# First two groups of chunks: fp32 operands, unscaled K, and products with T and A on 32x32 tiles

## The chip, the cores and the metric

The kernel runs on one core of a Trainium2 chip. The metric is device time in microseconds (us), smaller is better; the median of several runs counts. The engines are PE (TensorE: matmuls and weight loads), DVE (VectorE), ACT (ScalarE), POOL (GpSimd) and SP, which here only issues DMA transfers. "us" of an engine are its busy time in a profiled execution.

## The reference

A delta-rule attention over 4 batches x 8 heads, 768 tokens, 48 dimensions per head, followed by a gated feed-forward network on its output:

```python
k_n = k / (np.linalg.norm(k, axis=-1, keepdims=True) + 1e-06)
state = np.zeros((B, H, D, D))
for t in range(S):
    y[:, :, t] = q[:, :, t] @ state                    # per head
    v_old = state^T k_n[:, :, t]
    state = state + beta_t * outer(k_t, v_t - v_old)
x = y as [B*S, H*D] = [3072, 384]
out = ((x @ w_a) * (x @ w_b)) @ w_out                  # w_a, w_b: 384 x 1536, w_out: 1536 x 384
```

All inputs and outputs are fp32. Only the recurrence over t is sequential; the network works on each token alone.

## The kernel before, in words

**Chunks and groups.** The 768 tokens are cut into 24 chunks of 32 tokens, and the chunks into 6 groups of 4. The 32 pairs of batch and head are worked on at once: 4 blocks of 32 partitions times 8 column blocks q. Within a chunk the recurrence is replaced by products: with A the strictly lower triangle of Q K^T, and T the inverse of a unit triangular matrix made from K K^T times the strengths beta, a chunk takes the old state S, forms `ks` = K S, then vt = V - ks, then u = T vt, then `yp` = Q S + A u, and adds K^T u to the state in PSUM (`S_ps`). So each chunk waits for the state of the chunk before.

**Three stages per group.** `prep(g)` computes the squares and norms of K and Q, loads K and Q with tokens along the columns (`kqt` into `raw`), multiplies K there by the reciprocal of its norm (`rbk` or its slice `rb`, spread over the partitions: in group 0 by a matmul, in the others through a small array `rk` in DRAM), lays K and Q out in block-diagonal tiles `kqbd`, and makes the products K K^T and K Q^T (in the trace `raw,kqbd` for fp32, `kqc,kqbd` for fp16). `solve(g)` inverts the triangular matrices with 31 short VectorE steps (group 0: 15 steps on two halves at once, then small matmuls `b,ta`, `b,mk` and `wr,b`). `steps(g)` walks through the chunks: `shl` is the copied state, `khl` K with tokens along the partitions, `uhl` u, `t` vt, `y` the output of the chunk. The matmul with T is `t,tabd` (fp32) or `fhl,tabd` (fp16), the one with A is `uhl,tabd`. `tabd` is a block-diagonal 128x128 copy of the 32x32 matrices, made from the tile `ta` by copies on ScalarE and VectorE, whose split the table `COPY` holds ('AVAV': one letter per piece). Those of `kqbd` come likewise.

**Precision.** In general every attention operand is split into two fp16 halves, high and low, and a product is a sum of three fp16 products (`parts(g)`). Groups with `WIDE[g]` = 1, before this change group 0 alone, use fp32 operands and one product instead; a tile in fp32 takes the room of its two fp16 halves (`half`, `ta32`, `tas32`). The low half of a tile is made by one VectorE instruction, or, where `VIA_PE` names it by letter, by a matmul with a negative identity `neg` (in the trace `raw,mk` and `kqc,neg`, `t,mk` and `khl,neg`) whose result ScalarE copies. `LO_W` does the same for the three column thirds of the weights ('P': matmuls `wsl,zi` and `wsl,neg`; 'V': VectorE).

**The feed-forward stage.** `weights(p)` decodes a third of the weights and splits it into high and low fp16 halves (`wsl`, `wos`). Two chunks together make one piece of x (256 tokens, `x`), and `moe(s, ths)` runs per block of 128 hidden columns 18 matmuls 128x256 (`x,wsl`), ACT and DVE instructions that make the gate `g` and its halves `ghl`, and 6 matmuls 128x384 (`wos,ghl`). The latter come `LAG` blocks later. There are 144 such blocks.

**What sets the order.** No engine's order stands in the source. `Plan` records every operation, prices each (`price`), links them by what they read and write, and places them by list scheduling with priorities (`URGENCY` by stage) under several settings, of which it issues the one that it reckons shortest. Every instruction is issued at one line, and so has L476 in the trace. Each engine, and SP's queue of transfers, runs its instructions in that fixed order; an instruction that waits holds up those behind it. The pool of 6 PSUM banks and the rings of tiles (`raw`, `t`, `b`, `tabd`) are shared among the stages.

## Time and profile before

| | |
|---|---|
| median of 3 runs | 673.44 us (672.57 to 675.61) |
| profiled execution: device time, span | 675.9 us, 674.1 us |
| PE, DVE, ACT, POOL busy | 621.5, 545.0, 400.2, 11.5 us |
| first product of the first solve on PE | at 58.85 us |
| first MoE matmul on PE | at 107.95 us |
| first MoE matmul with x of the second group | at 215.52 us |

Times are of one profiled execution, in us from the start of its span. A row of groups reads: line, engine, operation, output <- inputs, shapes, count, then busy time in us and the mean of one in ns, then the idle time just before and what released it. A row of the timeline reads: start, length, engine, operation, count, idle before it. An fp32 matmul leaves two matmul records or one, by its form, so counts of records are not counts of calls. `PEclk` is the granted clock of PE as a share of full speed, in tenths in the slices of the page.

### The profile page before, as it was taken

The numbers are of one execution on the slowest core, as the hardware profiler recorded it, in microseconds if no ns is written. First come the engines' busy times: TensorE is split into PE (matmuls) and PEld (weight loads), VectorE is DVE, ScalarE is ACT, GpSimd is POOL, SyncE is SP. The second block draws the span as 40 slices with busy tenths as digits, with TensorE's granted clock in tenths as the row PEclk, the third lists the DMA queues.
The fourth block names the chain that finished last, engine by engine and source line by source line (L and its number), as shares of the span: only waits on it lengthen the run. The fifth ranks groups of instructions, "written<-read, shape, count | busy, mean of one in ns | idle before, by whom it ended". The sixth has DMA issues, their size and how long they took to land.

```text
span 674.1 us, 24273 instructions
## 1 busy us (share of the span) xinstructions
PE 621.5 (92%) x10578; PEld 495.0 (73%) x10578; DVE 545.0 (81%) x1532; ACT 400.2 (59%) x968; POOL 11.5 (2%) x15
## 2 busy tenths in 40 slices
PE   0748989999989999999999999999999999999997
PEld 0524878787777888777777778888777878887885
DVE  5999669899998799989999798899897898644232
ACT  9679548975387565477733876525657235553332
POOL 0000011100000000000000000000000000000000
PEclk9967659999999999989999999999999999999999
DMA  8997635512231432202420023001222000000000
GB/s 313 342 328 220 197 119 176 157 52 71 64 97 47 141 95 76 59 26 78 135 63 25 3 83 104 26 1 44 83 65 63 13 13 27 26 26 1 13 13 23
DMA packets 30243, 59.10 MB, mean 88 GB/s; under 512 B 3386, under 2 KB 21050, under 8 KB 30138
## 3 DMA queue, kind: packets, MB, share of 16 engines
q1 hardware_dynamic: 30138, 57.57, 27.2%
q8 instruction: 82, 1.34, 0.9%
q14 instruction: 23, 0.19, 0.1%
HBM read 52.75 MB, written 4.80 MB: 85 GB/s over the span
## 4 chain that ended last, share of the span: by engine, by line
PE 49%; DVE 32%; ACT 10%; DMA 6%; issue 2%; DVEq 0%; ACTq 0%; SPq 0%
PE bank L476 47%; DVE b L476 6%; DVE tmp L476 4%; DMA raw<-in_kqt 3%; DVE g L476 3%; DVE ghl L476 2%; DVE wsl L476 2%; DVE kqc L476 2%; ACT kqbd L476 2%; ACT tabd L476 2%; PE S_ps L476 2%; DVE t L476 2%; DVE wos L476 1%; DVE shl L476 1%; ACT t L476 1%
## 5 line engine op out<-in xcount | busy, mean ns | idle before, releaser
L476 PE MATMUL bank<-x,wsl 128*128 128x256 f16 x2592 | 309.8, 273 | 1.0 <-DVE x L476 0.8
L476 PEld LDWEIGHTS <-wsl 128*128 128x128 f16 (+1 forms) x2676 | 255.5, 98 | 61.1 <-DVE wsl L476 16.6
L476 PE MATMUL bank<-wos,ghl 128*128 128x384 f16 x864 | 165.3, 327 | 1.4 <-issue 1.2
L476 PEld LDWEIGHTS <-ghl 128*128 128x128 f16 x864 | 81.5, 98 | 41.3 <-issue 0.8
L476 ACT CAST ghl<-g 128x256 f16<-128x256 f32 x144 | 58.4, 405 | 83.5 <-DVE g L476 82.5
L476 ACT ACTIVATE a<-bank,rsc 128x256 f32<-128x256 f32 x120 | 56.8, 473 | 76.9 <-PE bank L476 76.3
L476 DVE TENSOR_TENSOR g<-bank,a 128x256 f32<-128x256 f32 x144 | 60.4, 420 | 47.3 <-ACT a L476 46.9
L476 DVE TENSOR_TENSOR ghl<-g,ghl 128x256 f16<-128x256 f32 x144 | 60.4, 419 | 17.6 <-ACT ghl L476 17.1
L476 PEld LDWEIGHTS <-kqbd 112*64 112x64 f16 x2880 | 51.6, 114 | 15.7 <-issue 13.4
L476 DVE TENSOR_TENSOR b<-b,tmp 128x31 f32<-128x31 f32 (+20 forms) x170 | 56.3, 331 | 2.1
L476 DVE TENSOR_TENSOR tmp<-b 128x31 f32<-128x31 f32 (+20 forms) x170 | 56.1, 330 | 2.1
L476 PE MATMUL bank<-shl,kqbd 112*64 112x48 f16 (+1 forms) x2112 | 46.6, 195 | 2.1 <-DVE shl L476 1.7
L476 ACT ACTIVATE t<-bank 128x96 f32<-128x96 f32 x96 | 22.6, 249 | 22.6 <-PE bank L476 22.1
L476 PEld LDWEIGHTS <-tabd 128*128 128x128 f16 x960 | 28.6, 96 | 7.9 <-issue 4.4
L476 DVE COPY tabd<-ta 32x1024 f16<-32x1024 f16 (+1 forms) x64 | 26.8, 419 | 5.9 <-ACT ta L476 3.0
L476 ACT COPY tabd<-ta 32x1024 f16<-32x1024 f16 (+1 forms) x32 | 29.7, 930 | 0.4
L476 ACT ACTIVATE t<-bank,y 128x96 f32<-128x96 f32 x96 | 25.6, 343 | 7.1 <-DVE y L476 7.0
L476 PE MATMUL bank<-uhl,tabd 128*128 128x48 f16 (+1 forms) x544 | 27.1, 203 | 2.4 <-issue 1.9
L476 ACT ACTIVATE ld<-ld 128x1536 f32<-128x1536 f32 x15 | 22.3, 1488 | 9.2 <-DMA ld<-in_vn 5.1
L476 PE MATMUL S_ps<-uhl,khl 32*48 32x48 f16 (+1 forms) x2080 | 23.6, 191 | 2.1 <-issue 1.9
L476 DVE COPY kqbd<-kqc 48x2048 f16<-48x2048 f16 x32 | 21.9, 684 | 1.8 <-PE bank L476 1.5
L476 PE MATMUL bank<-wsl 128*128 128x128 bf16 (+1 forms) x84 | 8.2, 236 | 15.9 <-DVE wsl L476 15.9
(154 smaller groups left out, 789.4 us busy)
## 6 DMA issues: line engine op xcount, KB each, us to landing
raw<-in_kqt SPq DMA_DIRECT2D x21, 448.0 KB, 3.7
rbk<-rk SPq DMA_DIRECT2D x40, 128.0 KB, 3.1
t<-in_kn SPq DMA_DIRECT2D x24, 192.0 KB, 2.7
stage<-in_wo SPq DMA_DIRECT2D x6, 768.0 KB, 5.8
out<-wsl SPq DMA_DIRECT2D x24, 192.0 KB, 1.9
ld<-in_kn SPq DMA_DIRECT2D x5, 768.0 KB, 7.8
ld<-in_qtok SPq DMA_DIRECT2D x5, 768.0 KB, 5.5
ld<-in_vn SPq DMA_DIRECT2D x5, 768.0 KB, 6.2
```

The source lines that it names most:

```text
L476: fn(*(self.place(a, lease) for a in args), **{k: self.place(a, lease) for k, a in kw.items()})
```

## The change

- The second group joins the first in `WIDE`: fp32 operands, one product in place of three.
- In both, T and A are multiplied as 32x32 tiles straight from the tile `ta` (`TILED_T`, in `ta_of`), so that no block-diagonal copies `tabd` are made for them.
- K stays unscaled there. The squares of the reciprocal norms go into the strengths (`bs`), and v is multiplied by the factors `r` (`vt`) with `ks` added afterwards; the product with the broadcast reciprocals goes, and with it the detour over DRAM of group 1 and the matmul of group 0. `k32` is loaded straight into `khl`. The inverse gets a factor of 2^18 that keeps its range.
- `VIA_PE` is empty, and `LO_W` is 'VVV': all low halves come from VectorE.
- `LAG` is 3 in place of 2. `COPY` is set anew for K of group 0, T of groups 1 and 4. Priorities of `prep0` and `steps1` rise.
- In the planner, the prices of fp32 matmuls change, and the transfers with a rank (`first_of`) go first on SP's queue, in the order of their ranks, with all the others behind.

```diff
@@ -30,30 +30,34 @@
-COPY = {'k': ['AA', 'AA', 'VV', 'VV', 'VV', 'VV'], 'ta': ['AVAV', 'AVAV', 'AVAV', 'AVAV', 'VVVV', 'VVVV']}
+COPY = {'k': ['VV', 'AA', 'VV', 'VV', 'VV', 'VV'], 'ta': ['AVAV', 'AVVV', 'AVAV', 'AVAV', 'AVAV', 'VVVV']}
 TILED_K = [0, 0, 0, 0, 0, 0]
-TILED_T = [0, 0, 0, 0, 0, 0]
-VIA_PE = ['aknu', 'kn', '', '', '', '']
+TILED_T = [1, 1, 0, 0, 0, 0]
+VIA_PE = ['', '', '', '', '', '']
...
-WIDE = [1, 0, 0, 0, 0, 0]
+WIDE = [1, 1, 0, 0, 0, 0]
+TILED_G = [0, 0, 0, 0, 0, 0]
 WD = 512
-LO_W = 'PVV'
-LAG = 2
+LO_W = 'VVV'
+LAG = 3
 LEAD = 4
-URGENCY = {'w0': 100, 'w0b': 800, 'w1': 300, 'w2': 300, 'prep0': 1000, 'solve0': 400, 'steps0': 300, 'prep1': 600, 'solve1': 200, 'steps1': 100, 'prep': 200, 'solve': 600, 'steps': 500, 'moe': 800, 'moe_pe': 300}
+URGENCY = {'w0': 100, 'w0b': 800, 'w1': 300, 'w2': 300, 'prep0': 1100, 'solve0': 400, 'steps0': 300, 'prep1': 600, 'solve1': 200, 'steps1': 200, 'prep': 200, 'solve': 600, 'steps': 500, 'moe': 800, 'moe_pe': 300}
 class Op:
-    __slots__ = ("eng", "calls", "dur", "move", "rd", "wr", "deps", "pri", "at", "end", "tag", "stream", "banks", "cold", "use", "many")
+    __slots__ = ("eng", "calls", "dur", "move", "rd", "wr", "deps", "pri", "at", "end", "tag", "stream", "banks", "cold", "use", "many", "rank")
...
         self.cold, self.use, self.many = 0.0, 0.0, 0
+        self.rank = None
         self.rd, self.wr, self.deps, self.tag, self.banks = {}, {}, set(), "", set()
@@ -74,6 +78,11 @@
         self.behind = set()
+        self.rank = None
+    def first_of(self, rank):
+        self.rank = rank
@@ -169,11 +178,13 @@
                 if ins[0].dtype == F32:
-                    return n if k <= 32 else 1.3 * n
+                    return 28.0 if k <= 48 else 66.0
                 return 10.0 if k <= 32 else 19.0
...
                 return 34.0 + n / 2.4
-            return (max(n, 60) / 2.4 + 2.3) * (4 if ins[0].dtype == F32 else 1)
+            if ins[0].dtype == F32:
+                return (max(n, 134) / 2.4 + 2.3) * 4
+            return max(n, 60) / 2.4 + 2.3
         if eng == "ACT":
...
@@ -414,7 +428,8 @@
             for k, late in nxt[i]:
-                ready[k] = max(ready[k], end + late)
+                ready[k] = max(ready[k], stop[i] if late is None else end + late)
                 left[k] -= 1
@@ -449,6 +464,14 @@
                 self.pred[i].append((j, late))
+        front = sorted((i for i, o in enumerate(ops) if o.rank is not None), key=lambda i: ops[i].rank)
+        for i, k in zip(front, front[1:]):
+            self.succ[i].append((k, None))
+            self.pred[k].append((i, None))
+        for k, o in enumerate(ops):
+            if o.eng == "SP" and o.rank is None:
+                self.succ[front[-1]].append((k, None))
+                self.pred[k].append((front[-1], None))
         best = None
...
@@ -806,6 +827,8 @@
     def ta_of(g, c, rows, which, l, q):
+        if WIDE[g] and TILED_T[g]:
+            return tas32(c, which)[rows, q]
         if WIDE[g]:
@@ -835,10 +858,13 @@
         if g == 0:
+            plan.first_of(1)
             SP.dma_start(kn0, kn[0:4].rearrange("c p d -> p c d"))
...
             V.tensor_reduce(ss, kn0.rearrange("p c (q e) -> p (c q) e", e=D), AX.X, ALU.add)
+            plan.first_of(0)
             load_raw(0, raw0)
+            plan.first_of(2)
             SP.dma_start(raws[0:KR], kqt[1:4].rearrange("c d x -> d c x"))
@@ -857,14 +883,14 @@
         rT = rTt
-        V.transpose(rT, r)
-        if g == 0:
-            for t, e in zip(ar.tiles, (rch[:, 0:4], rch[:, 4:8])):
-                A.copy(t.rearrange("p (k d) -> p k d", d=64), e.unsqueeze(2).broadcast_to([P, 4, 64]))
-            V.tensor_mul(
-                rbk0, rT.unsqueeze(1).broadcast_to([P, 16, 32]), rpi.unsqueeze(2).broadcast_to([P, 16, 32])
-            )
+        if WIDE[g]:
+            bs = bsm[:, g * 32 : g * 32 + 32]
+            V.tensor_mul(r, r, r)
+            V.tensor_mul(bs, bs, r)
+            V.transpose(bun[:, g * 32 : g * 32 + 32], bs)
         else:
+            V.transpose(rT, r)
             rk = scr.tile([2, 32, 2, 32], F32, name=f"rk{g}")
@@ -892,6 +918,9 @@
         V.tensor_scalar_mul(sc[:, 0:1], sc[:, 5:6], -256.0)
+        if WIDE[g]:
+            V.tensor_scalar_mul(r, s1, sc[:, 0:1])
         if g:
@@ -909,26 +938,16 @@
                 load_raw(c, rw)
+            if not WIDE[g]:
                 src = rk[:, ci * 8 : ci * 8 + 8].rearrange("h u r t -> h (u r t)")
...
                     )
-            else:
-                rb = abr()
-                T.matmul(
-                    rb,
-                    ar.tiles[ci // 2][:, ci % 2 * P : ci % 2 * P + P],
-                    rbk0.rearrange("p a t -> p (a t)"),
-                    start=True,
-                    stop=True,
-                )
-                rb = rb.rearrange("p (a t) -> p a t", t=32)
             bd = kqbd[c % 4]
             if WIDE[g]:
-                V.tensor_mul(rw[0:KR, 0], rw[0:KR, 0], rb[0:KR])
                 b32 = kq32(c)
-                for k in range(2 if c else 1):
+                for k in range(2) if c else [0] * (not TILED_G[g]):
                     for h2 in range(2):
...
@@ -988,7 +1008,9 @@
         (G if g else V).memset(X, 0.0)
-        V.tensor_copy(X.rearrange("p t s -> p (t s)")[:, 0 : 33 * 31 + 1 : 33], bun[:, g * 32 : g * 32 + 32])
+        V.tensor_scalar_mul(
+            X.rearrange("p t s -> p (t s)")[:, 0 : 33 * 31 + 1 : 33], bun[:, g * 32 : g * 32 + 32], 2.0**18 if WIDE[g] else 1.0
+        )
         size = 16 if HALVES[g] else 32
@@ -1064,16 +1086,13 @@
             bd, ta, tab = kqbd[c % 4], tas[c], tabd[c % 2]
-            kn32 = s15()
             khl = khr()
-            k32 = half(khl) if WIDE[g] else kn32
-            SP.dma_start(kn32, kn[c])
-            V.tensor_mul(
-                k32.rearrange("p (q e) -> p q e", e=D),
-                kn32.rearrange("p (q e) -> p q e", e=D),
-                r[:, ci * 8 : ci * 8 + 8].unsqueeze(2).broadcast_to([P, 8, D]),
-            )
+            k32 = kn32 = half(khl) if WIDE[g] else s15()
+            SP.dma_start(k32, kn[c])
+            rb = r[:, ci * 8 : ci * 8 + 8].unsqueeze(2).broadcast_to([P, 8, D])
+            by_heads = lambda t: t.rearrange("p (q e) -> p q e", e=D)
             if not WIDE[g]:
+                V.tensor_mul(by_heads(kn32), by_heads(kn32), rb)
                 k2 = khl.rearrange("p l q e -> p l (q e)")
@@ -1096,9 +1115,11 @@
             f32 = vt
-            if first:
+            if WIDE[g]:
+                V.tensor_mul(by_heads(vt), by_heads(v0), rb)
+            elif first:
                 A.activation(vt, v0, AF.Copy, scale=sc[:, 5:6])
-            else:
+            if not first:
                 if ci == 0:
@@ -1119,7 +1140,10 @@
                         )
-                V.scalar_tensor_tensor(vt, v0, sc[:, 0:1], ks[:, 0:384], op0=ALU.mult, op1=ALU.add)
+                if WIDE[g]:
+                    V.tensor_add(vt, vt, ks[:, 0:384])
+                else:
+                    V.scalar_tensor_tensor(vt, v0, sc[:, 0:1], ks[:, 0:384], op0=ALU.mult, op1=ALU.add)
             fhl = None if WIDE[g] else fhr()
@@ -1144,7 +1168,7 @@
             if WIDE[g]:
-                A.activation(u32, up[:, 0:384], AF.Copy, scale=2.0**-10 if first else -(2.0**-18))
+                A.activation(u32, up[:, 0:384], AF.Copy, scale=-(2.0**-18))
             else:
...
```

SP's queue, first rows, before:

```order
L476 DMA wsl<-in_kn 128x4x384
L476 DMA b_70<-in_wa 128x1024
L476 DMA stage<-in_wa 128x2x1024
L476 DMA ld_75<-in_kn 128x4x384
L476 DMA b_70<-in_wb 128x2x1024
L476 DMA mk<-in_masks 128x444
L476 DMA raw_110<-in_kqt 112x1024
L476 DMA wsl<-in_kqt 112x3x1024
```

and after (`kqt` are K and Q, `kn` K with tokens along partitions, `wa` and `wb` weights):

```order
L499 DMA raw_111<-in_kqt 112x1024
L499 DMA wsl<-in_kn 128x4x384
L499 DMA wsl<-in_kqt 112x3x1024
L499 DMA b_70<-in_wa 128x1024
L499 DMA stage<-in_wa 128x2x1024
L499 DMA b_70<-in_wb 128x2x1024
L499 DMA t_0_71<-in_beta 128x192
L499 DMA acc<-in_vn 128x4x384
L499 DMA mk<-in_masks 128x420
```

K and Q of the first four chunks have moved from behind the weights to the front, and the masks behind them.

PE, in the steps of the first group's early chunks, before (`bank_...` are the PSUM banks; the shapes are those of the outputs):

```order
L476 MATMUL bank_66<-b_70,ta_82 32x16 x32
L476 MATMUL bank_67<-b_70,mk 128x256
L476 MATMUL bank_65<-raw_110,mk 112x512
L476 MATMUL bank_64<-t_3_74,tabd_107 128x48 x8
L476 MATMUL bank_67<-wr_144,b_70 16x16 x32
L476 MATMUL bank_68<-uhl_151,tabd_107 128x48 x8
L476 MATMUL S_ps<-uhl_151,khl_145 48x48 x32
L476 LDWEIGHTS neg_117
L476 MATMUL bank_65<-kqc_80,neg_117 112x512
```

and after:

```order
L499 MATMUL S_ps<-uhl_152,khl_146 48x48 x32
L499 MATMUL bank_66<-b_70,ta_83 32x16 x32
L499 MATMUL bank_64<-shl_148,kqbd_105 64x48 x16
L499 MATMUL bank_68<-b_70,mk 128x256
L499 MATMUL bank_67<-uhl_152,ta_81 32x48 x32
L499 MATMUL bank_65<-t_1_72,ta_82 32x48 x32
L499 MATMUL bank_66<-b_70,ta_84 32x16 x32
L499 LDWEIGHTS mk
L499 MATMUL bank_67<-y_0_123,mk 128x4
```

The 8 products with `tabd`, each over the whole array, have become 32 products of 32x32 tiles with `ta`; the products `raw,mk` and `kqc,neg`, which made low halves for the second group, are no longer there.

More of the change, by code (lines that the diff above doesn't have):

```diff
@@ L215, in add @@
         if eng == "SP":
+            op.rank, self.rank = self.rank, None
             op.dur = 430.0
@@ L232, in add @@
                 else:
-                    op.cold += max(outs[0].shape[-1] if len(outs[0].shape) == 2 else 64, 48) / 1.2 * (4 if ins[0].dtype == F32 else 1)
+                    wide = ins[0].dtype == F32
+                    n = outs[0].shape[-1] if len(outs[0].shape) == 2 else 64
+                    op.cold += max(n, 131 if wide else 48) / 1.2 * (4 if wide else 1)
         for regs, aps in ((op.wr, outs), (op.rd, ins)):
@@ L526, in tile_kernel @@
     one = lambda name, shape, dt=F32: cst.tile(shape, dt, name=name)
-    mk = cst.tile([P, 60 + 3 * P], F32, name="mk")
+    mk = cst.tile([P, 36 + 3 * P], F32, name="mk")
     SP.dma_start(mk, masks)
@@ L532, in tile_kernel @@
     ones = mk[:, 32 : 32 + P]
-    rpi, rch = mk[:, 32 + 2 * P : 48 + 2 * P], mk[:, 48 + 2 * P : 56 + 2 * P]
-    same = mk.bitcast(BF16)[:, 2 * (56 + 2 * P) + 1 : 2 * (56 + 3 * P) : 2]
-    rown = mk[:, 56 + 3 * P : 60 + 3 * P]
+    same = mk.bitcast(BF16)[:, 2 * (32 + 2 * P) + 1 : 2 * (32 + 3 * P) : 2]
+    rown = mk[:, 32 + 3 * P : 36 + 3 * P]
     wsl = cst.tile([P, 19, 512], F32, name="wsl")
@@ L756, in heads, with pairs @@
                     yield q, i, l, rr, h4, slice(q * D, q * D + D)
-    def pairs(g):
+    def pairs(g, tiled=None):
         for q in range(8):
@@ L764, in pairs @@
                     cols = slice(q * D, q * D + D)
-                    if TILED_K[g]:
+                    if TILED_K[g] if tiled is None else tiled:
                         for h2 in range(2):
@@ L954, in prep @@
             with plan.group():
-                for q, i, l, rr, pr, rows, to, _ in pairs(g):
+                for q, i, l, rr, pr, rows, to, _ in pairs(g, TILED_G[g] if WIDE[g] else None):
+                    a = q * 2 + pr
                     T.matmul(
                         ga[to, q, :],
-                        kq_of(g, c, rows, l, q * 2 + pr, 0),
-                        rw[0:KR, :, q * 2 + pr] if WIDE[g] else kqc[rows, rr, q * 2 + pr],
+                        rw[rows, 0, a] if TILED_G[g] and WIDE[g] else kq_of(g, c, rows, l, a, 0),
+                        rw[rows, :, a] if WIDE[g] else kqc[rows, rr, a],
                         start=(i == 0),
@@ L1223, in steps @@
             if WIDE[g] and not WIDE[g + 1]:
-                G.memset(half(bd).rearrange("p (x n) -> p x n", n=64)[:, :, 16:48], 0.0)
-                if ci >= len(chs) - 2:
+                if c or not TILED_G[g]:
+                    G.memset(half(bd).rearrange("p (x n) -> p x n", n=64)[:, :, 16:48], 0.0)
+                if ci >= len(chs) - 2 and not TILED_T[g]:
                     G.memset(half(tab).rearrange("p (x n) -> p x n", n=128)[:, :, 16:112], 0.0)
@@ L1410, in _layout @@
                 perm[j * 128 + hp * 32 + e] = ((cc // D) * 4 + hp) * D + cc % D
-    masks = np.zeros((P, 60 + 3 * P), np.float32)
+    masks = np.zeros((P, 36 + 3 * P), np.float32)
     masks[:, 0:32] = np.tile(np.triu(np.ones((32, 32), np.float32), 1), (4, 1))
@@ L1415, in _layout @@
     masks[:, 32 + P : 32 + 2 * P] = np.eye(P, dtype=np.float32)
+    masks[:, 32 + 2 * P : 32 + 3 * P] = np.tile(np.eye(32, dtype=np.float32), (4, 4))
     row = np.arange(P)
-    masks[row, 32 + 2 * P + row % 8 * 2 + row // 64] = 1.0
-    masks[row, 48 + 2 * P + row // 8 % 4 * 2 + row // 32 % 2] = 1.0
-    masks[:, 56 + 2 * P : 56 + 3 * P] = np.tile(np.eye(32, dtype=np.float32), (4, 4))
-    masks[row, 56 + 3 * P + row // 32] = 1.0
+    masks[row, 32 + 3 * P + row // 32] = 1.0
     return {
```

## The prediction

> **What bounds the kernel now.** I read the page first: busy time, the slices, the granted clock.
>
> ```profile
> span 674.1 us, 24273 instructions
> PE 621.5 (92%) x10578; PEld 495.0 (73%) x10578; DVE 545.0 (81%) x1532; ACT 400.2 (59%) x968; POOL 11.5 (2%) x15
> PE   0748989999989999999999999999999999999997
> PEclk9967659999999999989999999999999999999999
> ```
>
> PE is busy in 621.5 of 674.1 us and idle mostly at the start; its clock is low in the third to sixth slice. Next the busy time by stage. The boundaries are the first product of the first solve (58.8), the first MoE matmul (107.9) and the first matmul of the second group's MoE (215.4).
>
> ```profile
> 0.00:20.00 20.00, 3.06 (x17) 1.96 (x18) 11.73 (x25) 18.91 (x33) 0.20 (x4) 1.00 0.91 309
> 20.00:57.00 37.00, 25.03 (x207) 13.85 (x206) 35.34 (x110) 26.82 (x39) 0.95 (x1) 0.82 0.98 328
> 58.80:107.90 49.10, 45.18 (x977) 38.41 (x977) 34.52 (x100) 30.94 (x70) 1.90 (x2) 0.63 0.53 164
> 107.90:215.40 107.50, 103.09 (x1627) 82.21 (x1626) 101.32 (x308) 76.80 (x175) 5.62 (x5) 1.00 0.30 92
> 215.40:674.10 458.70, 444.31 (x7764) 358.49 (x7758) 360.25 (x989) 244.88 (x651) 2.85 (x3) 0.99 0.16 49
> 187.00:215.00 28.00, 24.60 (x695) 18.96 (x695) 23.89 (x64) 23.34 (x58) 0.95 (x1) 1.00 0.26 76
> 140.00:187.00 47.00, 46.59 (x386) 37.12 (x384) 47.00 (x150) 24.87 (x54) 0.00 (x0) 1.00 0.16 49
> 300.00:320.00 20.00, 19.18 (x599) 15.50 (x597) 18.62 (x49) 15.33 (x46) 0.00 (x0) 1.00 0.25 74
> ```
>
> The columns are window, length, busy time (and records) of PE, weight loads, DVE, ACT, POOL, then granted clock, DMA share, GB/s. There are four regimes. Before 58.8 VectorE and the DMA are full (35.34 of 37 us, DMA share 0.98) and PE waits for the first solve. From 58.8 to 107.9 PE is busy for 45.18 of 49.10 us at a granted clock of 0.63, with small products. From there PE is at 96 to 97%; but from 140 to 187, while the second solve runs, VectorE has 47.00 of 47.00 us, so both bind. So the end is the start of the solve's products, plus the stretch ahead of the MoE, plus PE's work after it. The change touches all three.
>
> The profiled execution took 675.9 us with a span of 674.1, so 1.8 lie around it; the runs' median is 673.44, 2.5 below that execution. I sum against the span and set the result against the median.
>
> **Term 1, up to 58.8.**
>
> ```profile
> 6.84 0.43 DVE L476 TENSOR_SCALAR wsl<-b 128x512 int32<-128x512 int32 x1 [5.13 <-DMA b<-in_wa]
> 54.35 1.24 DVE L476 STREAM_TRANSPOSE b<-b 128x1024 f32<-128x1024 f32 x1
> 58.34 0.58 PE L476 MATMUL bank<-wsl,neg 128*128 128x512 f16 x1 [0.88 <-ACT wsl L476]
> 58.85 1.05 PE L476 MATMUL bank<-b,ta 32*32 32x16 f32 x64
> L476 DVE TENSOR_TENSOR wsl<-wsl,bank 112x512 f32<-112x512 f32 x3 | 2.0, 653 | 0.0
> raw<-in_kqt SPq DMA_DIRECT2D x21, 448.0 KB, 3.7
> wsl<-in_kqt SPq DMA_DIRECT2D x1, 1344.0 KB
> ```
>
> K and Q of the first four chunks (448 + 1344 = 1,792 KB) now go ahead of w_a. At 309 GB/s that delays w_a by 5.8 us, so its first decode starts near 12.6. VectorE, which is full here, loses the multiplications of K (three at 0.65, a fourth like them, the broadcast product: 3.3 us) and gains eight copies of K from ScalarE, 5.2 us at the same 0.65: +1.9. The solve's last transposition ends at 55.6 now, and PE's first product of it starts only at 58.85, behind `wsl,neg`, which waits for ScalarE. That product of the weights goes, so up to 3.2 us of lateness costs nothing here; 5.8 + 1.9 that isn't made good would cost 4.5. K is loaded before the weights and the first solve needs no K that is scaled, which can only bring it forward. Bounds -3 and +6; I take +1.
>
> **Term 2, 58.8 to 107.9.** The groups of this window, and single rows of the timeline:
>
> ```profile
> L476 PE MATMUL bank<-t,tabd 128*128 128x48 f32 x48 | 9.1, 366 | 0.0
> L476 PE MATMUL bank<-uhl,tabd 128*128 128x48 f32 x32 | 7.3, 415 | 0.0
> L476 PE MATMUL bank<-raw,mk 112*112 112x512 f32 x4 | 3.9, 1085 | 0.0
> L476 PE MATMUL bank<-wsl,neg 128*128 128x512 f16 x3 | 1.8, 606 | 0.9 <-ACT wsl L476 0.9
> L476 PE MATMUL bank<-kqc,neg 112*112 112x512 f16 x2 | 1.3, 654 | 0.0
> L476 PE MATMUL bank<-kqc,kqbd 112*64 112x64 f16 x96 | 2.4, 219 | 0.0
> 24.26 1.15 PE L476 MATMUL bank<-raw,kqbd 112*64 112x64 f32 x32
> 74.69 1.53 PE L476 MATMUL S_ps<-uhl,khl 32*48 32x48 f32 x64
> 112.99 0.93 PE L476 MATMUL S_ps<-uhl,khl 32*48 32x48 f32 x64
> 86.39 0.43 PE L476 MATMUL bank<-wr,b 32*16 32x16 f32 x30 [3.26 <-issue]
> 107.95 2.13 PE L476 MATMUL bank<-x,wsl 128*128 128x256 f16 x18
> ```
>
> The six groups all leave or change form: 9.1 + 7.3 + 3.9 + 1.8 + 1.3 + 2.4 = 25.8 us. In come the products with T and A on 32x32 tiles. Their nearest row is the state's product, also 32 fp32 tiles of 48 columns: 1.53 us for 64 records at the low clock, 0.93 at the full one. Three T and two A products (48 and 32 records of 16) thus become 5 x 1.53 = 7.7. Two products of K with K and Q, fp32 instead of three fp16 products, come at 1.15 each, 2.3. PE's work is then 45.2 - 25.8 + 10.0 = 29.4 us: 49.1 - 29.4 = 19.7 less if PE never waits for its instructions.
>
> But the records grow: 185 leave, 5 x 64 + 2 x 32 = 384 come, so some 1,180 matmuls, and as many weight loads: 2,350 records in place of 1,954. The densest sustained stretch of the trace is 300 to 320, 599 + 597 records in 20 us, 16.7 ns each. At that rate 2,350 take 39 us. The trace also shows PE idle for 3.26 us with the releaser "issue" in the middle of the densest run of small tiles. So the stretch lies between 29 (work) and 49 us (nothing gained); I take 39, **-10**.
>
> The Trainium skill's page "Runtime: NRT & Kernel Launch", section "Instruction fetch mechanics", says that the sequencer fetches blocks of 256 instructions ahead of itself and that this is mostly hidden; by that rule the stretch would be PE's own work, -20. The stall of 3.26 us speaks against the rule here, which is why it is a rival below.
>
> The cover of small products here is nothing: no MoE matmul can run before 107.95, so each us of waiting is one of the span.
>
> **Term 3, 107.9 to 215.4.**
>
> ```profile
> L476 PE MATMUL bank<-uhl,tabd 128*128 128x48 f32 x32 | 4.0, 277 | 0.0
> L476 PE MATMUL bank<-t,tabd 128*128 128x48 f32 x18 | 2.4, 277 | 0.0
> L476 PE MATMUL bank<-t,mk 128*128 128x384 f32 x8 | 3.3, 499 | 0.3 <-DVE g L476 0.3
> L476 PE MATMUL bank<-khl,neg 128*128 128x384 f16 x4 | 1.3, 334 | 0.0
> L476 PE MATMUL bank<-raw,mk 112*112 112x512 f32 x2 | 1.0, 593 | 0.0
> L476 PE MATMUL bank<-shl,kqbd 112*64 112x48 f16 x240 | 4.7, 190 | 0.0
> L476 PE MATMUL bank<-shl,kqbd 112*64 112x48 f32 x96 | 3.4, 224 | 0.0
> L476 DVE COPY tabd<-ta 32x1024 f16<-32x1024 f16 x56 | 23.4, 418 | 1.4 <-PE bank L476 0.2
> L476 DVE SCALAR_TENSOR_TENSOR kqc<-raw,sc,kqc 112x512 f16<-112x512 f32 x20 | 14.9, 746 | 0.1
> L476 DVE TENSOR_TENSOR raw<-raw,rbk 112x512 f32<-112x512 f32 x20 | 13.8, 689 | 6.1 <-DMA raw<-in_kqt 4.8 <-DMA rbk<-rk 1.2
> ```
>
> The first five go: 12.0 us. Three tile products at the full clock come, 2.8. For the second group the two products per chunk that read the state become fp32: a chunk's fp32 product takes 3.4 / 3 = 1.13 us (96 records are three of 32), the three fp16 terms together 4.7 / 5 = 0.94 (240 are five of 48), so 0.4 more per chunk and 1.2 for the three chunks that lie in this stretch. The products of K with K and Q get 0.75 cheaper per chunk at most (a chunk's 96 fp16 records against 32 of fp32); I leave that as a reserve against the switching between tiles and whole-array matmuls, which no row prices. Net -12.0 + 2.8 + 1.2 = -8.
>
> VectorE must follow, since it is full from 140 to 187. It loses, for the second group: eight copies of block-diagonal tiles (8 x 0.42 = 3.4), four multiplications of K (4 x 0.69 = 2.8), four low halves of K and Q (4 x 0.75 = 3.0): 9.2 us. The low halves of the state, of u and of the strengths go as well; at K's 0.75, an estimate, two per chunk are 6 more. It gains the weights' low halves of one third, 4 x 0.75 = 3.0. Net -12, more than PE's -8, so VectorE does not become the only bound. PE's idle time here, 107.50 - 103.09 = 4.4, is mostly at the hand-over between the groups, where the chain per chunk loses its hi and lo splits; I take 3 of it off. Bounds: -12.4 (all the idle goes) and 0 (the chain over VectorE as long as now). **-11.**
>
> **Term 4, 215.4 to the end.** The last of the second group's chunks with fp32 operands cost +1. Group 4's copies of T and A move in part to ScalarE (244.88 busy of 458.70, room enough), and the second MoE half lags three chunks instead of two. PE's idle time is 14.4 us in all; the changed order may take or give 3. **+1.**
>
> **Sum.** +1 - 10 - 11 + 1 = -19 on 674.1 gives a span of 655; against the median, 673.4 - 19 = **654**.
>
> **The rivals.** (a) *The stretch ahead of the MoE gains nothing.* Another product starts each time that an earlier one has been read by VectorE or ScalarE; if that chain, or the instructions (2,350 records at 21 ns, the 49 us over 2,350), set the length now, its 19.7 us of PE's work turn into waiting. For it: the "issue" idle of 3.26 us. Against it: PE is busy 45.18 of 49.10. Then +1 + 0 - 11 + 1 = -9: 664. Chance 0.20.
>
> (b) *PE's work counts in full*, no limit by records: +1 - 19.7 (45.2 to 29.4, and the 3.9 of idle) - 12.4 + 1 = -30: 643, or 640 where term 4 gives its 3. For it: at 58.85, 64 matmuls and as many loads take 1.05 us, 8 ns a record, with no stall. Against it: that is a short burst. Chance 0.13.
>
> (c) *Slower: the clock in the hand-over.* From 58.8 to 107.9, small products run at a granted clock of 0.63 though PE is busy. Where group 1's steps now come on 32x32 tiles, the same could befall the MoE's matmuls beside them: 18 matmuls of 128x256 take 2.13 us at full clock, and double that at half. The window from 187 to 215, where the first group hands over, holds 24.6 us of PE's work; at half clock throughout it would take 24.6 more: 674.1 - 19 + 24.6 is 6 over now, 679 by the median. It decides from 19 us of such work. Against it: from 107.9 on the clock is 0.99 to 1.00, small products included, since they lie between matmuls of 128 rows. Chance 0.05. The Trainium skill's page "TensorE: Matmul & The Clock Gate", section "Part 1: The HAM clock gate", has the clock halved after an idle window of about 3.4 us and free after a busy one; the row of 0.63 with PE at 92% busy shows more than that rule tells, so the rule alone would leave (c) out.
>
> (d) *The new order loses what it gains*: groups 2 to 5 are ordered anew around the shifted start, and PE idles 15 to 19 us more there, twice its 14.4 us now: 670 to 677. Chance 0.05.
>
> **How the numbers follow.** The forecast, 645 to 661, has 0.57; (a) 0.20, (b) 0.13, (c) 0.05, (d) 0.05. The range takes in (a) with the upper half of its spread and (b): 640 to 668. Within 0.5% of the median (670.1 to 676.8, about what a measurement of this kernel tells from no change) lies most of (d): 0.05. Slower by more is (c): 0.05. Faster: 0.90.
>
> **What would show it right or wrong.** The first MoE matmul near 99 (term 1 and 2 together; 108 would be (a), 89 (b)); idle of PE with the releaser "issue" in that stretch of 5 us or more (the record limit); the first MoE matmul of the second group near 196; granted clock 0.99 from there on (0.8 or less: (c)); and PE's idle time after it near 14 us (30: (d)). The forecast is wrong if the first MoE matmul comes on time and the end doesn't.

## The result and the profile after

The changed kernel takes 665.1 us (663.98 to 669.92), the kernel before 674.5 in the same comparison: a ratio of 0.9874, 95% interval 0.9825 to 0.9923. It is faster by 9 us, not by 19. The forecast of 654 was wrong: the time lies within the outer range, 640 to 668, but outside the forecast's own case, 645 to 661, and the gain is half of what was forecast. The profiled execution of the changed kernel took 665.2 us with a span of 663.4, so it stands for its median; the span fell by 10.7.

The page after, with the lines that answer to those shown of before:

```profile
span 663.4 us, 24797 instructions
PE 596.2 (90%) x10912; PEld 480.9 (72%) x10912; DVE 527.5 (80%) x1493; ACT 370.1 (56%) x923; POOL 8.8 (1%) x13
PE   3534878799998899999999999999999999999997
PEclk9655578999999999999999999999999999999999
```

PE's busy time fell by 25 us, the span by 11. Some 7 us of the 25 were products ahead of the first solve (the digits of PE's first slices), where PE waits anyway. Where the rest stands is told by the same two stages in both kernels: from the first product of the solve to the first MoE matmul, and from there to the end. Before:

```profile
58.85:107.95 49.10, 45.18 (x978) 38.46 (x978) 34.52 (x101) 30.94 (x70) 1.90 (x2) 0.63 0.53 163
107.95:674.10 566.15, 547.35 (x9379) 440.65 (x9378) 461.52 (x1296) 321.63 (x825) 8.48 (x8) 1.00 0.19 57
```

After:

```profile
59.63:101.70 42.07, 33.90 (x1162) 28.11 (x1163) 35.24 (x101) 23.82 (x58) 0.95 (x1) 0.58 0.64 201
101.70:663.40 561.70, 540.51 (x9512) 435.58 (x9508) 444.13 (x1239) 307.43 (x804) 7.62 (x8) 1.00 0.19 55
```

The second of these stages falls in two, which terms 3 and 4 of the prediction forecast: from the first MoE matmul to the first with x of the second group (in either kernel after 24 blocks of 18 matmuls; at 215.5 before and 208.4 after), and from there to the end. Before:

```profile
107.95:215.52 107.57, 103.16 (x1628) 82.25 (x1627) 101.39 (x308) 76.87 (x175) 5.62 (x5) 1.00 0.30 92
215.52:674.10 458.58, 444.19 (x7757) 358.41 (x7752) 360.13 (x989) 244.76 (x651) 2.85 (x3) 0.99 0.16 49
```

After:

```profile
101.70:208.42 106.72, 98.95 (x1780) 79.50 (x1777) 88.38 (x275) 59.08 (x153) 2.86 (x3) 0.99 0.29 86
208.42:663.40 454.98, 441.56 (x7739) 356.08 (x7732) 355.75 (x965) 248.35 (x651) 4.76 (x5) 1.00 0.16 48
```

The span is the start of the solve's products, plus PE's busy and idle time in each stage. "Forecast" is the sum of the prediction, put in the same form; the last column is a variant of the changed kernel with the same work in another order, which the experiments come to:

| us | before | forecast | after | same work, other order |
|---|---|---|---|---|
| first product of the solve (term 1) | 58.9 | 59.9 | 59.6 | 56.5 |
| ahead of the MoE (term 2): PE busy | 45.2 | 29.4 | 33.9 | 28.9 |
| ahead of the MoE: PE idle | 3.9 | 9.6 | 8.2 | 10.7 |
| MoE of the first group (term 3): PE busy | 103.2 | 95.2 | 99.0 | 99.4 |
| MoE of the first group: PE idle | 4.4 | 1.4 | 7.8 | 6.2 |
| from there to the end (term 4): PE busy | 444.2 | 445.2 | 441.6 | 442.6 |
| from there to the end: PE idle | 14.4 | 14.4 | 13.4 | 9.5 |
| span | 674.1 | 655.1 | 663.4 | 653.8 |

(The forecast's 95.2 is 103.2 less the 8 of term 3, its 1.4 is 4.4 less 3, its 445.2 is 444.2 plus the 1 of term 4.) The largest miss is the stage of term 3: it was to get 11 us shorter and got 0.9 shorter, for 3.8 us of PE's work and 6.4 us of idle time more than forecast. Term 2 misses by 3, with 4.5 us more of PE's work. Term 4 gave 4.6 us more than forecast.

What PE waited for behind the first MoE matmul, before:

```profile
PE bank L476 <- issue: 3.1, 2, 1.9
PE S_ps L476 <- issue: 1.9, 2, 1.1
PE bank L476 <- ACT t L476: 1.7, 3, 0.9
PE bank L476 <- DVE shl L476: 1.7, 3, 0.8
PE bank L476 <- DVE fhl L476: 1.6, 4, 0.7
```

After (us in total, times, the longest):

```profile
PE bank L499 <- ACT t L499: 3.5, 5, 1.2
PE bank L499 <- DVE t L499: 3.0, 2, 1.8
PE bank L499 <- DVE shl L499: 2.8, 2, 1.7
PE bank L499 <- ACT uhl L499: 2.0, 2, 1.4
```

These are waits in the steps of the chunks: for the output's squares and for vt (both `t`), the copied state and u. In PE's order MoE matmuls follow one or a few products behind them; that those could have run in the meantime is a reading, which no row shows. In the stage of term 3 alone, the waits for such steps grew from 1.1 us to 5.4.

### The profile page after: what moved, and what is told of

Its sections match the earlier page's. It is cut to its first block, busy times and chain, and to the rows that moved or that the text cites. A ratio compares the mean times of both kernels' runs of the same rounds, so it can differ in the third digit from the quotient of the medians.

```text
span 663.4 us, 24797 instructions
## 1 busy us (share of the span) xinstructions
PE 596.2 (90%) x10912; PEld 480.9 (72%) x10912; DVE 527.5 (80%) x1493; ACT 370.1 (56%) x923; POOL 8.8 (1%) x13
## 4 chain that ended last, share of the span: by engine, by line
PE 40%; DVE 36%; DMA 13%; ACT 9%; issue 2%; SPq 0%; DVEq 0%; ACTq 0%
PE bank L499 39%; DVE b L499 6%; DMA raw<-in_kqt 5%; DVE tmp L499 4%; DVE wsl L499 4%; DMA stage<-in_wa 3%; DVE g L499 3%; DVE ghl L499 3%; DVE t L499 2%; DVE wos L499 2%; DVE kqc L499 2%; ACT kqbd L499 2%; DMA stage<-in_wb 1%; DMA stage<-in_wo 1%; ACT t L499 1%
## 5 line engine op out<-in xcount | busy, mean ns | idle before, releaser
L499 PEld LDWEIGHTS <-wsl 128*128 128x128 f16 (+2 forms) x2676 | 256.3, 99 | 61.2 <-DVE wsl L499 11.0
L499 PE MATMUL bank<-shl,kqbd 112*64 112x48 f16 (+1 forms) x1984 | 48.6, 201 | 4.2 <-DVE shl L499 2.8
L499 PEld LDWEIGHTS <-kqbd 112*64 112x64 f16 x2304 | 39.8, 113 | 12.1 <-issue 10.9
L499 ACT ACTIVATE t<-bank,y 128x96 f32<-128x96 f32 x96 | 25.7, 347 | 13.9 <-DVE y L499 13.5
L499 PEld LDWEIGHTS <-tabd 128*128 128x128 f16 x768 | 22.9, 96 | 3.0 <-issue 0.7
L499 ACT COPY tabd<-ta 32x1024 f16<-32x1024 f16 x24 | 24.9, 1036 | 0.2
L499 PE MATMUL bank<-wsl 128*128 128x128 bf16 (+1 forms) x84 | 10.2, 268 | 12.7 <-DVE wsl L499 8.6
L499 ACT ACTIVATION_READ_ACCUMULATOR t<-bank 128x1 f32 x96 | 19.6, 205 | 0.0
L499 ACT ACTIVATE wsl<-wsl,sw 128x512 f16<-128x512 f32 x18 | 13.0, 721 | 11.5 <-DVE wsl L499 6.5
```

The lines of the kernel that those rows point to most:

```text
L499: fn(*(self.place(a, lease) for a in args), **{k: self.place(a, lease) for k, a in kw.items()})
```

## The experiments

Kernels are named by their labels. Unless said otherwise each is the changed kernel with one edit. Ratios are to the kernel before, timed beside them; the changed kernel itself, run again unaltered, gave 0.986 (0.9807 to 0.9913) and 0.989 (0.9862 to 0.9917). Stages are those of one profiled execution; the three of the changed kernel have spans of 658.8 to 663.8 us, so a difference of some 2 us in a stage can be chance. And the planner lays out every variant anew, so that each can have an order of its own.

### Undoing parts: one_wide, via_tabd, no_front, lo_p

```diff
-WIDE = [1, 1, 0, 0, 0, 0]                 # one_wide
-TILED_T = [1, 1, 0, 0, 0, 0]
+WIDE = [1, 0, 0, 0, 0, 0]
+TILED_T = [1, 0, 0, 0, 0, 0]
...
-TILED_T = [1, 1, 0, 0, 0, 0]              # via_tabd
+TILED_T = [0, 0, 0, 0, 0, 0]
...
-        front = sorted(...)               # no_front
+        front = []
...
-LO_W = 'VVV'                              # lo_p
+LO_W = 'PVV'
```

> Undoes the part of the change for the second group: it has fp16 halves, scaled K and block-diagonal copies again, all else as changed. Theory A (the second group's fp32 form relieves VectorE, which was full from 140 to 187 us, and its product form costs PE about 2 us: 25.7 us in the changed kernel, by its groups, against 23.7 for the same products in fp16): VectorE gets 12 us back there, the time rises by 5 to 10, to 670 to 675 us. Theory B (the second group's part earns nothing, its steps only make PE wait: 13.5 us of idle from 101.7 to 302.2 in the changed kernel, 5.8 in the comparable stretch before): 656 to 665 us, and the idle time there falls to 6 to 8.

> Undoes the 32x32 tiles alone: T and A of both groups go through block-diagonal fp32 copies over the whole array. Theory A (PE's work is what the tiles save): the first group's 16 products of 22.4 records-by-time in the old kernel (11.3 + 11.1 us) come back in place of 8.6, the second group's eight at 2.0 each in place of 0.9: +23 us, 685 to 690 us. Rival (the stretch ahead of the MoE is set by the chain over ScalarE and VectorE, so that dearer products fill waiting time): only the part behind the first MoE matmul counts, 672 to 678.

> Undoes the order of the transfers alone: K and Q of the first chunks are loaded where the planner puts them. Theory A (as in the prediction's term 1, the order of the transfers is worth 1 us either way): first product of the solve at 58 to 61 us, 664 to 667 us. Rival (the early K is what keeps the solve's start at 59.6 now that VectorE has more to do ahead of it): first product at 62 to 65 us, 668 to 671.

> Undoes one setting: the low halves of the first third of the weights come from PE again (about 9 us of products ahead of the solve, 1.8 behind it), VectorE loses four instructions of 0.75 us. Theory A (PE is idle ahead of the solve, so that only what lies behind it counts): 664 to 667 us. Rival (VectorE is what sets the solve's end and the first MoE matmul, so its 3 us count): 661 to 663.

Measured: one_wide 668.6 us (0.9940; 0.9918 to 0.9962), via_tabd 680.0 (1.0112; 1.0076 to 1.0149), no_front 664.5 (0.9881; 0.9837 to 0.9924), lo_p 669.7 (0.9942; 0.9910 to 0.9974).

The tiles carry the change: without them the rest is slower than the kernel before. In via_tabd the products with T and A over the whole array take, in both groups,

```profile
L499 PE MATMUL bank<-t,tabd 128*128 128x48 f32 x128 | 20.5, 325 | 4.1 <-ACT tabd L499 3.1 <-DVE t L499 0.9
L499 PE MATMUL bank<-uhl,tabd 128*128 128x48 f32 x128 | 17.5, 294 | 0.0
```

38.0 us, against the tiles' 17.2 in the changed kernel:

```profile
L499 PE MATMUL bank<-t,ta 32*32 32x48 f32 x512 | 8.9, 230 | 4.8 <-DVE t L499 3.0 <-ACT ta L499 1.7
L499 PE MATMUL bank<-uhl,ta 32*32 32x48 f32 x512 | 8.3, 212 | 2.1 <-ACT uhl L499 2.0
```

The two stages of via_tabd:

```profile
59.97:108.33 48.36, 41.89 (x932) 37.35 (x933) 38.45 (x109) 29.12 (x67) 0.95 (x1) 0.61 0.55 179
108.33:675.70 567.37, 553.78 (x8972) 448.39 (x8970) 450.55 (x1255) 310.40 (x807) 10.38 (x10) 0.99 0.18 55
```

PE is busy there for 595.7 us from the solve on, 21.3 more than in the changed kernel, while its idle time is 20.1 in place of 29.4. So theory A had PE's work nearly right (23), but the time, 680, lies between its range and its rival's: of 21 us of work that the tiles save, 9 come back as waiting (12 us between the spans, 15 between the medians). This is the same exchange as between the kernel before and the changed one (18 us of work, 6.6 of them back).

The second group's part: one_wide is slower by 3 to 4 us. The two explanations both miss, since 668.6 lies between their ranges. PE's work from the solve on is 4 us less, but its idle time stays (30.7 us); and the solve's first product comes at 63.9 in place of 59.6. VectorE is full again from 140 to 187 us, as theory A had it (46.6 of 47 us, against 41.9 in the changed kernel), but PE is busy there for 45.7 us against 46.2, so VectorE holds it up little. The order of the transfers is worth nothing that can be measured, as expected, though the solve's first product came 2 us later, at 61.7. lo_p is slower where no change was expected; its idle time ahead of the MoE rose from 8 to 13 us, 5.5 of which are a single wait for VectorE (`zi`) just ahead of the first MoE matmul. Why that one is so long there stays open.

### Is the stretch set by the chain from chunk to chunk? chain0, chain1, no_a0

```diff
-                A.activation(u32, up[:, 0:384], AF.Copy, scale=-(2.0**-18))
+                for _ in range(5 if g == 0 else 1):          # chain0; chain1: g == 1
+                    A.activation(u32, up[:, 0:384], AF.Copy, scale=-(2.0**-18))
...
-                for q, i, l, rr, rows, cols in fours(g):     # no_a0, for yp
+                for q, i, l, rr, rows, cols in fours(g) if g or first else ():
```

> In the four chunks of the first group ScalarE copies u out of PSUM five times in place of once, about 0.5 us each: 2 us longer a chain from chunk to chunk, nothing more for PE. Theory A (ahead of the first MoE matmul PE waits for the chain over ScalarE and VectorE, so that cheaper products end there as waiting): three of the four chunks lie ahead of the first MoE matmul, which moves from 101.7 to about 107, idle there rises from 8 to 13 us, and the time rises by 5 to 8, to 670 to 673 us. Rival (the supply of PE's instructions or PE's own work sets the stretch, as the prediction had it): the first MoE matmul moves by less than 2 us and the time by less than 2.

> The same in the four chunks of the second group, where MoE matmuls of the first chunks stand ready to fill PE. Theory A (behind the first MoE matmul PE's work is the bound, and its waits there come from the order in which it was laid out, not from the length of the chain): the time rises by less than 2 us, 663 to 667. Rival (the chain from chunk to chunk sets this stretch too, from 101.7 to 237): 8 us longer a chain, 671 to 674.

> Leaves out the tile products with A in chunks 1 to 3 of the first group, which no later chunk waits for (so the output is another): about 1.5 us of PE's work and 128 records each at the low clock. Theory S (PE's instructions or work set the stretch ahead of the first MoE matmul): two of them lie there, so the stretch of 42 us gets 3 to 5 us shorter, and the time falls by 3 to 5, to 660 to 662. Rival (the stretch is set by what VectorE, ScalarE and the transfers deliver): 663 to 667.

Measured: chain0 666.5 us (0.9897; 0.9843 to 0.9951), chain1 664.6 (0.9888; 0.9828 to 0.9948), no_a0 662.8 (0.9848; 0.9803 to 0.9894).

By the times, a chain that is 8 us longer costs 1 or 2 us in the first group and nothing in the second, with some room: chain0's interval, 664 to 671 us, reaches the lower end of theory A's range, chain1's, 663 to 671, just meets that of its rival. In chain0's profile the first MoE matmul comes 4 us later, at 105.7, and PE is idle for 14.1 us ahead of it, as theory A had it, but not by waiting for the chain: PE never waited there for u, and it shows

```profile
PE bank L499 <- issue: 7.4, 4, 3.0
PE S_ps L499 <- issue: 2.4, 1, 2.4
```

9.8 us of idle time ahead of the MoE in which PE waited for no other engine. In chain1, PE's idle time behind the first MoE matmul is 16.5 us, less than the 21.2 of the changed kernel. So a longer chain need not lengthen the waits; that its length is of no account isn't shown, since the planner knew of the copies and could lay out other work beside them.

no_a0 takes away PE's work that nobody waits for; the stretch gets 3.1 us shorter,

```profile
59.24:98.20 38.96, 29.89 (x1028) 24.82 (x1028) 33.11 (x94) 22.95 (x56) 0.95 (x1) 0.58 0.63 205
```

which is what theory S expected of the stretch: PE's work is 4.0 us less there, its idle time 0.9 more. The time, 2 us less, lies between the two forecasts, and its interval reaches into both.

### Two settings of the planner: lag2, old_price

```diff
-LAG = 3                                                      # lag2
+LAG = 2
...
-                    return 28.0 if k <= 48 else 66.0         # old_price, with the two other prices of fp32
+                    return n if k <= 32 else 1.3 * n
```

> Undoes one setting: the second MoE half lags two blocks in place of three. Theory A (the lag is worth nothing that can be measured; in the kernel before, with two, the products with ghl were hardly waited for, 1.4 us of idle before them): 663 to 667 us. Rival (with less PE work between them the longer lag is what hides VectorE's and ScalarE's part): 668 to 672, with idle before the products with ghl of 4 us or more.

> Undoes the new prices of fp32 matmuls alone, so that the same work is laid out in an order that the old prices give. Theory A (the order matters as much as the work: behind the first MoE matmul 13 us of idle are waits for instructions that come later than the order reckoned): the idle between the first MoE matmul and 302 us moves by 4 us or more, and the time with it, 668 to 674 us. Rival (the order is of no account, the time follows PE's work): 663 to 667.

Measured: lag2 669.3 us (0.9929; 0.9900 to 0.9958), old_price 672.0 (0.9961; 0.9932 to 0.9990). old_price has the same work as the changed kernel and almost the time of the kernel before: the order alone is worth 7 us here, as theory A said. Its idle time from the first MoE matmul to 302 us was not the place, though (13.6 us against 13.5). Most of it lay ahead of the MoE, where PE was idle for 12.9 us in place of 8.2, with 1.7 us less work; behind it,

```profile
104.02:669.70 565.68, 544.01 (x9603) 438.30 (x9601) 450.64 (x1248) 308.64 (x805) 7.61 (x8) 0.99 0.18 54
```

there are 3.5 us more of PE's work and 0.5 more of idle. lag2 has the time that its rival forecast, but not its sign: before the products with `ghl` PE was idle for 0.5 us. What its loss of 4 us comes from stays open.

### Do transfers come late? few_loads, b_few, moved310

In the changed kernel a decoding instruction of the weights stands ahead of the chain's on VectorE and waits:

```profile
115.27 0.36 DVE L499 TENSOR_SCALAR wos<-stage 128x384 int32<-128x384 int32 x1 [3.23 <-DMA stage<-in_wo]
```

and PE's product with T waits for vt behind it, 1.8 us. few_loads leaves out the loads of the second and third thirds of the weights, b_few does the same in the kernel before; moved310 lets the planner reckon transfers as slower.

```diff
+                if p == 0:                                   # few_loads, b_few
                     SP.dma_start(t_, w[j, :, col : col + WD].bitcast(I32))
...
-            if i % 2 == 0:
+            if i % 2 == 0 and p == 0:
...
-            op.move = max(n / 360.0, 20.0)                   # moved310
+            op.move = max(n / 310.0, 20.0)
```

> Leaves out the loads of the second and third thirds of the weights (9.2 MB of 58; their decoding goes on with what lies in the buffers, so the output is another). Theory D (in the changed kernel transfers come late for instructions that stand ahead of the chain's on VectorE and ScalarE: 13 us of waiting for transfers from 60 to 130 us, 0.2 us in the kernel before): these waits fall below 5 us, PE's idle time from the first product of the solve to 302 us from 21 to 14 or less, and the time to 655 to 660 us. Rival (the idle comes from the order and from PE's instructions): the waits for transfers go, the time stays at 663 to 667.

> The kernel before with the same loads left out. Theory D: there the transfers were in time behind 60 us, so little is won, 3 us at most: 670 to 674 us. Rival (the traffic slows either kernel alike, by the fetching of instructions or by sharing the memory): as much is won here as in the changed kernel, 664 to 669.

> The same work; only the planner reckons transfers at 310 bytes per ns in place of 360 (the first 59 us of both kernels show 314 to 317 GB/s). Theory D (decoding instructions that stand ahead of the chain's on VectorE wait for transfers that are later than reckoned): the waits for transfers on VectorE and ScalarE from 60 to 130 us fall from 7 to 13 us below 5, the time falls by 3 or more, to 662 or less. Rival (they are an effect beside the point): 663 to 668.

Measured: few_loads 659.2 us (0.9796; 0.9749 to 0.9842), b_few 668.2 (0.9932; 0.9900 to 0.9964), moved310 664.1 (0.9839; 0.9790 to 0.9888).

The waits for transfers went in few_loads (3.0 us from 60 to 130 us, 13.1 in the changed kernel), and the time fell by 6 us (from 664.8 of after_again, beside it), into theory D's range; but the kernel before, which had hardly any such waits, won 6 us (674.2 to 668.2) as well, as the rival had it. The two win in different ways, though: from the solve to 302 us, PE's idle time in few_loads fell from 21.7 to 17.6 us (14 was expected), while in b_few it did not fall (22.7 us from the solve to the end, as before). And in both the granted clock ahead of the MoE is higher than with the loads, 0.71 in place of 0.58 and 0.86 in place of 0.63; why, no run shows. So the loads cost either kernel about alike; some 4 us of the changed kernel's idle time may be theirs, but they don't explain why it gained less than forecast. moved310 tells nothing more: it is within the intervals of the changed kernel, and its waits for transfers rose to 16.6 us (VectorE alone 9.0 us for `wo`).

### The order: after_again, slack, slack_moved, b_slack

after_again is the changed kernel unaltered. slack changes the latency that the planner reckons from VectorE or ScalarE to a product on PE; slack_moved has this and the price of moved310; b_slack is the kernel before with the new latency.

```diff
-        return {"PE": 180.0}.get(b.eng, 130.0)
+        return {"PE": 600.0}.get(b.eng, 130.0)
```

> The changed kernel once more, unaltered, for its time beside the same runs of the kernel before and for a second profiled execution. If idle with the releaser issue ahead of the first MoE matmul belongs to the order, it is within 1 us of the 1.4 us of the first profile; if it is chance (it was 1.2 to 9.8 us in the variants), it differs by 2 us or more. Time 663 to 667.

> The same work; only the planner's latency from VectorE or ScalarE to a product on PE is 600 ns in place of 180, so that PE's order leaves more room before a product that waits. Theory O (behind the first MoE matmul PE waits because its order leaves too little room, and MoE matmuls that stand ready come later in it): idle from the first MoE matmul to 302 us falls from 11 to 13 us to 7 or less, and the time by 3 to 6, to 659 to 662 us. Rival (the waits are set by VectorE's and ScalarE's own work, which no order of PE shortens): idle 9 us or more, 663 to 668 us.

> Both settings together. Theory O with D: 656 to 660 us, idle from the first MoE matmul to 302 us 6 or less. Rival: 663 to 668 us.

> The kernel before with the latency of 600 ns. Theory O (in the kernel before PE's dearer products filled the waits: 5.8 us of idle from the first MoE matmul to 302 us): little is won, 671 to 676 us. Rival (more room in the order is a gain of its own that has nothing to do with the change): the time falls by as much as in the changed kernel, to 668 to 670.

Measured: after_again 664.8 us (0.9860; 0.9807 to 0.9913), slack 667.0 (0.9888; 0.9836 to 0.9939), slack_moved 659.8 (0.9749; 0.9680 to 0.9818), b_slack 681.4 (1.0103; 1.0022 to 1.0183).

In after_again the idle time with releaser issue ahead of the first MoE matmul was 4.3 us in place of 1.4: by what was expected, it is chance. slack did what theory O said of the waits, idle of 7.1 us from the first MoE matmul to 302 us in place of 13.5, and not what it said of the time: more products were put ahead of the first MoE matmul, which came at 112.9,

```profile
61.82:112.88 51.06, 39.51 (x1364) 33.44 (x1365) 39.77 (x116) 25.75 (x62) 0.95 (x1) 0.60 0.59 189
112.88:664.30 551.42, 537.52 (x9310) 433.48 (x9306) 439.82 (x1232) 305.11 (x798) 7.62 (x8) 0.99 0.18 54
```

so that what was won behind it (13.9 us of idle in place of 21.2) was lost ahead of it, where the clock is low. In the kernel before the same setting is a loss, which neither explanation had. With both settings the time fell. The two last runs settle whether that was chance; after5 is the changed kernel, both5 is slack_moved unaltered.

> The changed kernel, unaltered, beside the next. Both theories: 0.984 to 0.989 of the kernel before, 663 to 667 us.

> The setting of slack_moved once more (latency of 600 ns, transfers at 310 bytes per ns, the work unaltered). Theory O (the order holds the lost gain): 0.972 to 0.979 of the kernel before, 656 to 661 us, with PE's waits for VectorE and ScalarE behind the first MoE matmul at 3 us or less. Rival (the first run of it was chance): 0.982 to 0.988, 662 to 667.

Measured: after5 665.6 us (0.9890; 0.9862 to 0.9917), both5 656.0 (0.9760; 0.9731 to 0.9788). The intervals are apart: the same work in another order is 9.6 us faster than the changed kernel, 17 us faster than the kernel before, and 2 us from the forecast. The stages of both5:

```profile
56.52:96.10 39.58, 28.87 (x1067) 24.52 (x1068) 30.06 (x84) 23.79 (x59) 0.74 (x1) 0.62 0.66 216
96.10:653.80 557.70, 542.01 (x9615) 438.28 (x9612) 448.70 (x1264) 307.63 (x805) 7.83 (x9) 1.00 0.19 59
```

Against the changed kernel, the solve's products start 3.1 us sooner; 95 fewer records lie ahead of the first MoE matmul, and PE's work there is 5.0 less for 1.5 more behind it; and PE's idle time from the MoE on is 15.7 in place of 21.2. Its waits there for the steps of the chunks are a third to a half of those shown above:

```profile
PE bank L499 <- DVE t L499: 1.4, 2, 1.3
PE bank L499 <- ACT t L499: 1.3, 3, 0.8
PE bank L499 <- DVE shl L499: 1.2, 3, 0.4
```

Together they are below 4 us, where 3 or less was expected of all waits for the two engines; with the smaller ones they are more, so that part of the expectation is missed, while the time is as theory O had it. Which of the two settings does it was not separated further: neither does it alone.

## Why the prediction was wrong

**Term 1 held in its size.** The solve's first product came 0.8 us later, +1 was forecast, a choice between -3 and +6; PE waited 6.0 us for the solve there, so the lateness was no longer hidden behind the weights' product, which had gone. That K comes first in the transfers brings the start forward by 2 us (61.7 in no_front), which the time doesn't show.

**Term 2, mis-sized by 3 of 10 us.** The new products were priced rightly in sum: the tiles took 6.9 us for 7.7, the fp32 products with K 3.1 for 2.3, together 10.0. The step that failed is "PE's work is then 45.2 - 25.8 + 10.0 = 29.4 us". The 25.8 came from rows of groups, the 45.2 from the busy time, and these don't add up alike: matmuls overlap, so the groups of that window sum to 50.5 us where PE was busy for 45.2. In the changed kernel they sum to 36.4 for 33.9, so 2.8 us of what was subtracted had never been in the 45.2. The other 1.7 us are products that the change leaves as they are: they took 26.4 us by their rows in place of 24.7. Most got dearer, while the granted clock fell from 0.63 to 0.58, but not all (the state's product went from 277 to 242 ns), so that the clock is the likely cause and not a shown one. Before:

```profile
L476 PE MATMUL bank<-shl,kqbd 112*64 112x48 f32 x96 | 4.2, 252 | 0.0
L476 PE MATMUL bank<-wos 128*128 128x128 bf16 x12 | 0.8, 218 | 0.0
```

After:

```profile
L499 PE MATMUL bank<-shl,kqbd 112*64 112x48 f32 x96 | 5.5, 289 | 1.4 <-ACT shl L499 1.1 <-issue 0.3
L499 PE MATMUL bank<-wos 128*128 128x128 bf16 x12 | 1.7, 307 | 0.0
```

**The limit by records is not shown.** The 39 us for this stretch came near the 42 measured, but for another reason: of 8.2 us of idle only 1.4 had the releaser "issue", most of the rest waited for ScalarE. The prediction asked for 5 us or more. The stall is real but varies: the same kernel, three times profiled, shows 1.4, 4.3 and 1.0 us of it in this stretch, both5 shows 7.7 and is the fastest of all. The Trainium skill's page "Runtime: NRT & Kernel Launch", section "Instruction fetch mechanics", calls the cost of crossing into the next block mostly hidden; these rows agree for two of the three executions and not for the third, and they don't show that the stalls are fetches.

**Term 3 is the step that failed most: -11 was forecast, -0.9 came.** The first MoE matmul of the second group came at 208.4, not near 196. In the other two executions of the changed kernel this stage took 106.1 and 107.0 us, so it isn't chance. VectorE's part was right (13.0 us less work, 12 forecast). Two steps were not:

- "Net -12.0 + 2.8 + 1.2 = -8": PE's work fell by 4.2 us. The rows of groups of this window fell by 6.6 (from 116.1 to 109.5), so 2.4 of that is the overlap once more. The rest of the miss is in the main the tiles: eight such products lie in the stage, 7.8 us, where the sum took in three, 2.8; four of the eight stand in place of fp16 products of the second group, 3.4 us, that the sum left out.
- "I take 3 of it off", since the chain per chunk loses its hi and lo splits: PE's idle time rose by 3.4 us, with 4.3 us more of waits for the steps of the chunks. Shorter work on VectorE and ScalarE did not shorten these waits.

**Term 4 gave -3.6 in place of +1**, 2.6 us of PE's work and 1.0 of idle time. That PE's work from the first MoE matmul on fell by 6.8 us in all, with 7 forecast, is luck: term 3 fell short by nearly as much as term 4 exceeded.

**What the waits hang on.** On the order, at least in part: both5 has the same work and is 9.6 us faster. But it doesn't bear out the sum. Against the changed kernel it starts 3.1 us sooner, PE's work is 3.5 less and its idle time 3.0 less (5.5 less behind the first MoE matmul, 2.5 more ahead of it), and its stage of term 3 takes 105.6 us, 2 less than in the kernel before and not 11. The total comes near the forecast by other terms. That dear products used to fill the time until VectorE and ScalarE had delivered, and cheap ones leave PE waiting, fits via_tabd: with the dear products back, PE is idle for 3.2 us in the stage of term 3 in place of 7.8, and for 9 us less in all. But via_tabd has another order as well, so this isn't shown apart from the order, and why these waits grew stays open. What the sum did without saying so is to take the order as following the work.

**The rivals.** (a) had the right time, 664, by a wrong way: it left out the stretch ahead of the MoE altogether, which gained 7 us, and the loss lay behind it. (b) fell: the first MoE matmul came at 101.7, not 89, and the idle time rose. (c) fell: the clock was 1.00 from the first MoE matmul on, with small tiles beside it. The Trainium skill's page "TensorE: Matmul & The Clock Gate", section "Part 1: The HAM clock gate", has the clock free after a busy window, so that by it alone (c) would have been left out; the 1.00 agrees, the 0.58 of the stretch ahead, with PE busy for 81% of it, does not. (d) was the nearest in kind, an order that gives back part of the gain, but was given 0.05 and put in groups 2 to 5; from 302 us on the changed kernel idles less than the kernel before (7.7 us against 13.0).

## What to carry to other kernels

Where a program lays out the order of the work itself, removing work gives a new order, and here orders of the same work lay between 656 and 672 us, nearly as far apart as the gain that was forecast: sum the work, then ask what fills the waits that the dear instructions used to cover, and give the forecast the width of that spread. Subtract like from like: rows of groups overlap, and must not be taken off a busy time without that overlap. Compare the stages one by one, since a sum of terms can come out right where the terms don't. And when a change falls short, lay out the same work once more with other planner settings before calling its parts worthless.

## What the runs showed of the hardware

That small products ahead of the first MoE matmul run at a low clock was known from the profile before (0.63). With the new tiles they do so with PE busy for 81% of the time (33.9 of 42.07 us, clock 0.58). The full clock comes a little after the first MoE matmuls: the first nine took nearly twice as long as the next nine,

```profile
101.70 2.09 PE L499 MATMUL bank<-x,wsl 128*128 128x256 f16 x9
106.18 1.16 PE L499 MATMUL bank<-x,wsl 128*128 128x256 f16 x9
```

and over all that follows the clock is 1.00, tiles included. With two thirds of the weights' loads left out, the clock ahead of the MoE was higher, 0.71 and 0.86. And the idle time with no releaser is chance to a good part: one kernel gave 1.0 to 4.3 us of it in the same stretch.
